# The four bit steps of a weight set apart, and the prologue's hand-written order rewritten

## The chip, the cores and the metric

The kernel runs on one core of one Trainium2 chip. The metric is the device time of one execution in microseconds (us), the median of three runs.

## What is computed

Windowed attention with a second, pooled branch (the reference's `_attn_ref`), whose output is the input of a gated feed-forward layer (`_moe_ref`):

```python
k_sum = k.reshape(B, H, nb, 32, D).max(axis=3)
v_sum = v.reshape(B, H, nb, 32, D).mean(axis=3)
scores_l = where(|row - column| < 16, scale * q @ k.T, -1e9)
scores_s = scale * q @ k_sum.T + log(32)
a = softmax(concat([scores_l, scores_s]))            # + 1e-9 in the divisor
x = a @ concat([v, v_sum])                           # 4 x 8 heads x 768 x 64
out = (silu(x @ w_gate) * (x @ w_val)) @ w_out       # 3072 tokens, 512 -> 1536 -> 512
```

The weights arrive as 64-bit floats. The kernel takes them as pairs of 32-bit words and makes 32-bit floats of them on the chip.

## The kernel before

The 3072 tokens are worked in eight blocks `k` of 384 tokens (half a batch each). Attention of a block has four units `u` (two heads each). The feed-forward layer of a block has twelve slices `j` of 128 of the 1536 inner columns. For each (k, j), `gate` and `val` (line 499, twelve matmuls each, three terms of a split of 32-bit floats into a high and a low part) lead over `silu`, `mul`, `ah` and `al` to `down` (line 550, nine matmuls that add to three banks of the block).

The weights are loaded and converted once, in a prologue that also does the attention of blocks 0 and 1 and the feed-forward layer of block 0 and half of block 1. Weight slice (j, gv) holds gate and value columns together (1024 per partition), (j, o) the output rows (512); slices 0 and 11 have `g` and `v` apart. A slice takes these steps: `w_load` (the transfer, SP queue), `w_abs` (ScalarE, line 177), `w_clamp` (two VectorE instructions, lines 185 and 187, the second on the result of the first), `w_bits` (two more, lines 195 and 198, each on the result of the one before), `w_hi` (a rounding copy, line 152 on ScalarE or line 154 on VectorE) and `w_lo` (a subtraction, line 148, on VectorE or, where the order says `=p`, on GpSimd).

Attention unit (k, u): keys, queries and values are loaded (`kt`, `q`, `kw`, `vn`, `vw`), keys pooled (`pool`) and windows put together (`winA`, `winB`, `join`), then `scores` (line 383), the running minimum `ttr0`/`ttr1` (line 398), `exp0`/`exp1` (line 413), `rcp` (lines 430 and 431), `nrm` (line 435), `tr0`/`tr1` (line 449), `pt0`/`pt1`, `out` (line 473), `split` and `rest`, which give the high and low part (`xh`, `xl`) of the layer's input. `first_values` (line 362) pools the first values on TensorE.

`PROLOGUE` (line 68) lists all these steps in one hand-written order; a suffix `=a`, `=d` or `=p` names ScalarE, VectorE or GpSimd. The loop at line 627 issues them so, and lines 632 to 635 tie every instruction to the one before it on its engine. So each engine, and the SP queue that starts the transfers, works through its part of the list strictly in order, and a step that has to wait holds all that stands behind it on that engine. After the prologue, `put_attention` and `do` (lines 648 to 677) place the attention of later blocks between the matmuls of the layer.

Of the kernel before, what the change touches and what calls it, by code (L numbers as in the profile page):

```python
# [98 lines left out]
w_clamp(7,o) down(1,0) w_hi(6,gv)=d mul(1,1) w_lo(6,gv)=d ah(1,1)=a gate(1,2) al(1,1)=d w_abs(8,gv)  # L99
w_clamp(4,gv) val(1,2) w_clamp(8,gv) silu(1,2) w_bits(4,gv) down(1,1) mul(1,2) w_hi(4,gv)=d ah(1,2)=a gate(1,3)  # L100
w_bits(8,gv) val(1,3) silu(1,3) al(1,2)=d w_hi(8,gv)=a w_lo(4,gv)=d down(1,2) w_lo(8,gv)=d w_abs(5,gv) mul(1,3)
w_abs(9,gv) w_clamp(5,gv) gate(0,4) ah(1,3)=a w_lo(4,o)=d al(1,3)=d w_bits(5,gv) val(0,4) silu(0,4) w_bits(7,o)
down(1,3) w_hi(5,gv)=a mul(0,4) w_hi(7,o)=a w_lo(5,gv)=d gate(1,4) ah(0,4)=d w_abs(7,gv) w_lo(7,o)=d al(0,4)=d
# [627 lines left out]
```

## Time and profile before

| | before |
|---|---|
| median of three runs | 726.92 us (726.63 to 727.62) |
| the profiled execution | 727.39 us, its span 725.6 us |
| TensorE busy | 705.6 us, 97% of the span |
| VectorE, ScalarE, GpSimd busy | 295.4, 319.0, 136.7 us |
| moved by DMA | 62.02 MB |

The span is cut in stretches and each engine's busy time read in each. A timeline row is one instruction (or several alike) with its start, its duration, its engine, line, operation and tiles; in square brackets stands how long the engine had been idle before it and on what it waited. "PEclk" is the granted clock of TensorE as a share of its full speed.

### The profile page before, as it was taken

Reading aid. Unit: us, or ns where it says so; the run is one execution under the profiler, and the core shown is the slowest. Engines: PE = TensorE matmul, PEld = TensorE weight load, DVE = VectorE, ACT = ScalarE, POOL = GpSimd, SP = SyncE. Lnnn points to the kernel's source line nnn. Section 1 sums busy time; section 2 is a strip of 40 time slices with the busy share of each in tenths; the row PEclk is TensorE's granted clock in tenths of the full one; section 3 lists DMA queues with packets and bytes.
Section 4 is the critical chain, followed back from the end, with each engine's and each line's share of the span. In section 5 each row is a group of like instructions: output and inputs, shape, how many; then the busy total and the mean of one; then the engine's idle time right before and its main releaser. Section 6 shows DMA issues by size and latency. Waiting matters only on the chain.

```text
span 725.6 us, 12513 instructions
## 1 busy us (share of the span) xinstructions
PE 705.6 (97%) x4986; PEld 642.9 (89%) x4986; DVE 295.4 (41%) x840; ACT 319.0 (44%) x779; POOL 136.7 (19%) x150
## 2 busy tenths in 40 slices
...
PEclk8798999999999999999999999999999999999999
...
GB/s 292 351 357 373 93 1 1 95 34 126 182 163 110 66 44 44 45 111 47 64 89 110 67 44 44 15 74 44 45 45 45 84 5 17 2 38 7 1 1 43
DMA packets 56522, 62.02 MB, mean 85 GB/s; under 512 B 24272, under 2 KB 46480, under 8 KB 55184
## 3 DMA queue, kind: packets, MB, share of 16 engines
...
## 4 chain that ended last, share of the span: by engine, by line
PE 82%; DVE 13%; ACT 2%; issue 1%; DMA 1%; SPq 0%; ACTq 0%; DVEq 0%
PE v L499 25%; PE g L499 24%; PE acc L550 24%; PE xo L473 3%; PE sc L383 3%; PE pp L449 2%; DVE m_gv L195 1%; DVE m_gv L198 1%; DMA vn<-in_vP 1%; DVE al L148 1%; PE pv L362 1%; DVE a L511 1%; DVE w_gv L148 1%; DVE m_gv L185 1%; DVE m_o L195 1%
## 5 line engine op out<-in xcount | busy, mean ns | idle before, releaser
L499 PE MATMUL g<-xh,w_gv 128*128 128x384 f32 x640 | 179.4, 341 | 3.3 <-DVE w_gv L148 3.1
L499 PE MATMUL v<-xh,w_gv 128*128 128x384 f32 x640 | 180.2, 342 | 1.1 <-DVE a L511 1.0
L550 PE MATMUL acc<-w_o,ah 128*128 128x512 f32 x576 | 179.3, 392 | 0.0
L511 DVE TENSOR_TENSOR a<-v,a 128x384 f32<-128x384 f32 x96 | 53.4, 556 | 251.0 <-PE v L499 250.9
L148 POOL TENSOR_TENSOR al<-a,ah 128x384 fp32r<-128x384 f32 x78 | 79.1, 1015 | 259.0 <-ACT ah L152 259.0
L550 PEld LDWEIGHTS acc<-w_o,ah 128*128 128x128 f32 x576 | 108.0, 188 | 20.2
L499 PEld LDWEIGHTS g<-xh,w_gv 128*128 128x128 f32 x640 | 118.3, 190 | 6.5 <-DVE w_gv L148 3.5
L499 PEld LDWEIGHTS v<-xh,w_gv 128*128 128x128 f32 x640 | 117.7, 189 | 5.2 <-issue 2.4
L550 PE MATMUL acc<-w_o,al 128*128 128x512 f32 x288 | 114.5, 398 | 0.7 <-DVE al L148 0.7
L506 ACT ACTIVATE a<-g 128x384 f32<-128x384 f32 x96 | 47.2, 492 | 143.3 <-PE g L499 141.9
L499 PE MATMUL g<-xl,w_gv 128*128 128x384 f32 x320 | 108.5, 339 | 0.0
L499 PE MATMUL v<-xl,w_gv 128*128 128x384 f32 x320 | 108.1, 338 | 0.0
L152 ACT CAST ah<-a 128x384 fp32r<-128x384 f32 x91 | 46.4, 509 | 121.4 <-DVE a L511 121.4
L413 ACT ACTIVATE p<-p,nm 128x120 f32<-128x120 f32 x192 | 73.2, 382 | 0.6 <-DVE nm L398 0.3
L550 PEld LDWEIGHTS acc<-w_o,al 128*128 128x128 f32 x288 | 54.0, 188 | 11.6 <-DVE al L148 1.6
L499 PEld LDWEIGHTS g<-xl,w_gv 128*128 128x128 f32 x320 | 60.7, 190 | 2.5
L435 POOL TENSOR_TENSOR p<-p,ri 128x720 f32<-128x720 f32 x29 | 40.6, 1401 | 108.0 <-DVE ri L431 106.5
L499 PEld LDWEIGHTS v<-xl,w_gv 128*128 128x128 f32 x320 | 60.5, 189 | 0.0
L506 ACT ACT_TABLE_LOAD x27 | 34.6, 1283 | 53.9 <-PE g L499 53.7
L154 POOL COPY kw<-ks 128x144 f32<-128x144 f32 x25 | 7.6, 304 | 194.1 <-DVE ks L277 118.8
L398 DVE CUSTOM_DVE_ANT_0 p<-sc,bias_sb 128x120 f32<-128x120 f32 x192 | 41.2, 277 | 1.6 <-PE sc L383 1.5
L499 PE MATMUL g<-xh,w_g 128*128 128x384 f32 x128 | 36.1, 343 | 0.0
...
## 6 DMA issues: line engine op xcount, KB each, us to landing
...
```

The source lines that it names most:

```text
L148: (nc.vector if e == "d" else nc.gpsimd).tensor_tensor(out=out, in0=a, in1=b.bitcast(F32), op=ALU.subtract)
L152: nc.scalar.copy(out, in_)
L195: nc.vector.scalar_tensor_tensor(out=f, in0=high, scalar=-0x40000000, in1=f, op0=ALU.bitwise_and, op1=ALU.bitwise_or)
L383: nc.tensor.matmul(sc[h][s * QT : (s + 1) * QT, c * KC : (c + 1) * KC], t["q"][hs, qs], t["kw"][hs, i, :], start=True, stop=True,)
L398: nc.vector.tensor_tensor_reduce(out=t["p"][:, i, :], in0=t["sc"][g][:, c * KC : (c + 1) * KC], in1=bias_sb[:, 0 if n == 0 else 2 if n == ...
L413: nc.scalar.activation(out=t["p"][:, i, :], in_=t["p"][:, i, :], func=AF.Exp, scale=-1.0, bias=t["nm"][:, i : i + 1], accum_out=t["sm"][:, ...
L435: (nc.vector if on == "d" else nc.gpsimd).tensor_tensor(out=p, in0=p, in1=ri.rearrange("p (n o) -> p n o", o=1).broadcast_to([P, NT, KC]), ...
L473: nc.tensor.matmul(ps[hs, qs], vw, t["pt"][:, h, qs], start=True, stop=True)
L499: nc.tensor.matmul(ps[:, :TOK], w[:, cs], x, start=u == 0 and n == 0, stop=u == NP - 1 and n == 2)
L506: nc.scalar.activation(out=a, in_=A.pop(("g", k, j))[:, :TOK], func=AF.Silu)
L511: nc.vector.tensor_tensor(out=a, in0=ps[:, :TOK], in1=a, op=ALU.mult)
L550: nc.tensor.matmul(ACC[k][i], a[:, ts], w, start=j == 0 and n == 0, stop=j == NJ - 1 and n == 2)
```

## The change

`w_clamp` and `w_bits` are cut into four steps of one instruction each (`w_clamp`, `w_shift`, `w_sign`, `w_low`), and the addition of 1e-9 leaves `rcp` for a step `eps` of its own. The instructions are the same; the list can now put other work between them. The whole list is new: what stands where, on which engine the movable steps run, and in which order the SP queue starts the transfers. A step `dummy` (idle matmuls) is defined and not used in the list, and the tile `warm` moves to another pool. What comes after the prologue is not touched. The list below is cut after the first third, and its end is shown.

```diff
 PROLOGUE = """
-kt(1) q(0,3) q(0,1) kt(3) pool(1) winA(1)=a winB(1)=p bias() mean() vn(0) join(0,1)=a scores(0,1) pool(3)
-winA(3)=a winB(3)=a vn(2) ttr0(0,1) join(0,3)=a scores(0,3) ttr1(0,1) exp0(0,1) first_values(0) odd1(0)=d id()
-kt(0) ttr0(0,3) odd2(1)=p odd1(1)=p ttr1(0,3) exp1(0,1) q(0,0) odd2(0)=d kt(2) odd1(2)=p first_values(2)
-odd2(3)=a rcp(0,1) odd1(3)=a fv_copy(0)=d kw(1,1) nrm(0,1)=p exp0(0,3) fv_copy(1)=d pool(0) w_load(0,g)
-val1(0,1)=a winB(0)=p tr0(0,1) exp1(0,3) join(0,0)=d winA(0)=d tr1(0,1) vw(1,0) pool(2) val1(0,0)=p scores(0,0)
-val2(0,1)=p pt1(0,1)=a q(0,2) winB(2)=p fv_copy(2)=d pt0(0,1)=a rcp(0,3) w_load(1,gv) odd2(2)=a join(1,1)=d
-out(0,1) join(0,2)=d nrm(0,3)=p winA(2)=a ttr0(0,0) w_abs(0,g) ttr1(0,0) exp0(0,0) w_clamp(0,g) tr0(0,3)
-tr1(0,3) split(0,1)=d val1(0,2)=p scores(0,2) fv_copy(3)=a kw(1,0) values(1,0)=p val2(0,0)=a pt1(0,3)=d
-val1(0,3)=a rest(0,1) w_load(0,v) val2(0,3)=p exp1(0,0) pt0(0,3)=d w_bits(0,g) out(0,3) w_abs(1,gv) q(1,0)
-w_load(3,gv) rcp(0,0) ttr0(0,2) join(1,0)=p w_hi(0,g)=a nrm(0,0)=p split(0,3)=a ttr1(0,2) exp0(0,2) rest(0,3)
-w_lo(0,g)=d scores(1,0) exp1(0,2) w_clamp(1,gv) w_load(2,gv) tr1(0,0) tr0(0,0) val2(0,2)=a rcp(0,2) pt1(0,0)=a
-ttr0(1,0) nrm(0,2)=p pt0(0,0)=a ttr1(1,0) w_abs(0,v) out(0,0) exp0(1,0) vw(1,2) w_bits(1,gv) tr0(0,2) q(1,1)
-exp1(1,0) tr1(0,2) w_load(2,o) pt0(0,2)=a rcp(1,0) pt1(0,2)=a w_clamp(0,v) q(1,2) w_hi(1,gv)=a out(0,2)
-w_load(0,o) nrm(1,0)=d values(1,2)=a w_bits(0,v) tr1(1,0) split(0,0)=a tr0(1,0) room(0) w_load(10,gv)
-split(0,2)=a scores(1,1) rest(0,0) w_lo(1,gv)=p pt1(1,0)=a w_hi(0,v)=a pt0(1,0)=d rest(0,2) gate(0,0) w_abs(2,o)
-ttr0(1,1) w_abs(0,o) ttr1(1,1) exp0(1,1) kw(1,3) w_lo(0,v)=d w_load(8,o) out(1,0) w_clamp(0,o) exp1(1,1)
-w_clamp(2,o) val(0,0) w_load(1,o) silu(0,0) rcp(1,1) w_bits(0,o) kw(1,2) w_abs(3,gv) split(1,0)=d nrm(1,1)=p
-gate(0,1) vw(1,1) mul(0,0) rest(1,0) w_abs(2,gv) w_load(5,o) w_clamp(3,gv) ah(0,0)=a val(0,1) silu(0,1)
-w_clamp(2,gv) w_load(8,gv) join(1,3)=a join(1,2)=a values(1,1)=a al(0,0)=d w_hi(0,o)=a tr1(1,1) w_bits(2,gv)
-tr0(1,1) w_abs(1,o) scores(1,2) pt0(1,1)=a q(1,3) pt1(1,1)=a w_load(6,o) out(1,1) mul(0,1) w_lo(0,o)=p
-w_hi(2,gv)=a ttr0(1,2) w_load(6,gv) ttr1(1,2) split(1,1)=a down(0,0) exp0(1,2) rest(1,1) w_lo(2,gv)=d
-w_bits(2,o) gate(0,2) w_load(7,gv) exp1(1,2) w_clamp(1,o) w_hi(2,o)=a rcp(1,2) w_bits(1,o) val(0,2) ah(0,1)=a
-silu(0,2) w_load(3,o) nrm(1,2)=d w_bits(3,gv) tr1(1,2) w_hi(1,o)=a w_load(4,gv) tr0(1,2) pt1(1,2)=a scores(1,3)
-pt0(1,2)=a out(1,2) w_lo(1,o)=d w_hi(3,gv)=a al(0,1)=d vw(1,3) ttr0(1,3) split(1,2)=a down(0,1) w_lo(3,gv)=d
-w_load(7,o) exp0(1,3) rest(1,2) w_load(9,o) gate(0,3) ttr1(1,3) values(1,3)=p mul(0,2) exp1(1,3) w_load(4,o)
-ah(0,2)=d w_lo(2,o)=d val(0,3) w_abs(6,gv) rcp(1,3) al(0,2)=d w_load(10,o) nrm(1,3)=d w_abs(3,o) w_abs(7,o)
-w_clamp(6,gv) w_load(5,gv) tr1(1,3) silu(0,3) tr0(1,3) down(0,2) w_clamp(3,o) pt0(1,3)=d w_abs(4,o) pt1(1,3)=d
-w_abs(4,gv) mul(0,3) out(1,3) w_load(9,gv) w_bits(3,o) ah(0,3)=a split(1,3)=a al(0,3)=d w_hi(3,o)=a rest(1,3)
-gate(1,0) w_clamp(4,o) val(1,0) w_lo(3,o)=d silu(1,0) w_bits(4,o) w_abs(6,o) w_clamp(6,o) w_hi(4,o)=a down(0,3)
-mul(1,0) w_bits(6,o) gate(1,1) ah(1,0)=d w_hi(6,o)=d al(1,0)=d w_lo(6,o)=d w_bits(6,gv) val(1,1) silu(1,1)
 ...
-w_clamp(10,gv) val(0,7) silu(0,7) w_bits(10,gv) down(0,6) mul(0,7) w_hi(10,gv)=d ah(0,7)=a gate(0,8)
-w_lo(10,gv)=d al(0,7)=d room(1) w_load(11,v) val(0,8) silu(0,8) w_load(11,o) down(0,7) w_load(11,g) mul(0,8)
-ah(0,8)=a w_abs(11,v) al(0,8)=d w_clamp(11,v) gate(0,9) w_abs(11,o) w_bits(11,v) w_abs(11,g) w_clamp(11,o)
-val(0,9) silu(0,9) w_clamp(11,g) w_hi(11,v)=d w_bits(11,g) down(0,8) w_lo(11,v)=d w_hi(11,g)=a mul(0,9)
-w_lo(11,g)=d ah(0,9)=a gate(0,10) w_bits(11,o) al(0,9)=d w_hi(11,o)=d val(0,10) silu(0,10) w_lo(11,o)=d
 ...
+kt(1) q(0,1) kt(3) q(0,3) pool(1) winB(1)=a winA(1)=p bias() mean() vn(2) join(0,1)=d scores(0,1) pool(3)
+winB(3)=a winA(3)=a join(0,3)=d scores(0,3) kt(0) ttr0(0,1) ttr1(0,1) exp0(0,1) q(0,0) kt(2) ttr0(0,3)
+first_values(2) odd2(3)=p ttr1(0,3) odd1(3)=p id() vn(0) odd1(2)=p pool(0) exp1(0,1) winB(0)=p winA(0)=d
+join(0,0)=p exp0(0,3) eps(0,1) scores(0,0) winB(2)=d rcp(0,1) q(0,2) fv_copy(2)=d nrm(0,1)=d fv_copy(3)=a
+kw(1,1) odd2(2)=a pool(2) val2(0,3)=p exp1(0,3) tr1(0,1) w_load(0,g) val1(0,2)=p tr0(0,1) val1(0,3)=p ttr0(0,0)
+first_values(0) odd1(0)=a odd1(1)=p pt1(0,1)=d pt0(0,1)=a q(1,0) odd2(1)=p ttr1(0,0) exp0(0,0) kw(1,0) odd2(0)=p
+eps(0,3) winA(2)=d w_load(1,gv) rcp(0,3) exp1(0,0) join(0,2)=d nrm(0,3)=d scores(0,2) fv_copy(1)=d join(1,1)=p
+w_abs(0,g) fv_copy(0)=d val2(0,1)=p tr0(0,3) val1(0,1)=a eps(0,0) w_clamp(0,g) tr1(0,3) val2(0,2)=a rcp(0,0)
+out(0,1) ttr0(0,2) val1(0,0)=p val2(0,0)=a q(1,2) nrm(0,0)=p pt1(0,3)=a pt0(0,3)=d w_load(0,v) exp0(0,2)
+ttr1(0,2) out(0,3) split(0,1)=d join(1,0)=p exp1(0,2) w_shift(0,g) w_load(2,o) rest(0,1) tr1(0,0) scores(1,0)
+w_sign(0,g) pt1(0,0)=a eps(0,2) vw(1,0) split(0,3)=a w_low(0,g) tr0(0,0) w_abs(1,gv) rcp(0,2) q(1,1) rest(0,3)
+nrm(0,2)=p ttr0(1,0) vw(1,2) w_hi(0,g)=a ttr1(1,0) pt0(0,0)=a w_load(3,gv) exp0(1,0) tr1(0,2) w_clamp(1,gv)
+out(0,0) w_lo(0,g)=d exp1(1,0) w_shift(1,gv) tr0(0,2) w_sign(1,gv) w_abs(0,v) w_load(0,o) pt0(0,2)=a eps(1,0)
+pt1(0,2)=a w_clamp(0,v) rcp(1,0) values(1,2)=a w_shift(0,v) out(0,2) w_load(2,gv) nrm(1,0)=d values(1,0)=a
+w_low(1,gv) split(0,0)=a tr1(1,0) tr0(1,0) split(0,2)=a scores(1,1) pt1(1,0)=a w_sign(0,v) pt0(1,0)=a rest(0,0)
+w_hi(1,gv)=a room(0) w_load(10,gv) out(1,0) w_low(0,v) w_abs(0,o) rest(0,2) w_lo(1,gv)=p gate(0,0) ttr0(1,1)
+split(1,0)=a w_hi(0,v)=a rest(1,0) exp0(1,1) ttr1(1,1) kw(1,2) w_clamp(0,o) exp1(1,1) w_load(8,o) w_lo(0,v)=d
+w_shift(0,o) val(0,0) w_abs(2,gv) eps(1,1) w_sign(0,o) kw(1,3) rcp(1,1) w_low(0,o) silu(0,0) w_load(1,o)
+nrm(1,1)=d w_clamp(2,gv) w_load(3,o) tr1(1,1) w_hi(0,o)=a gate(0,1) mul(0,0) join(1,2)=p join(1,3)=a
+w_shift(2,gv) w_abs(2,o) w_load(7,o) w_lo(0,o)=d ah(0,0)=a pt1(1,1)=a w_sign(2,gv) scores(1,2) w_abs(1,o)
+vw(1,1) silu(0,1) w_clamp(1,o) tr0(1,1) w_abs(3,gv) w_low(2,gv) q(1,3) val(0,1) w_load(4,gv) pt0(1,1)=a
+ttr0(1,2) al(0,0)=p w_abs(3,o) ttr1(1,2) w_hi(2,gv)=a values(1,1)=p down(0,0) mul(0,1) exp0(1,2) w_shift(1,o)
+w_lo(2,gv)=d w_load(9,gv) out(1,1) w_sign(1,o) w_clamp(3,gv) exp1(1,2) gate(0,2) w_low(1,o) w_load(10,o)
+w_shift(3,gv) split(1,1)=a w_hi(1,o)=a eps(1,2) rest(1,1) ah(0,1)=a val(0,2) rcp(1,2) w_sign(3,gv) w_load(7,gv)
+silu(0,2) nrm(1,2)=d al(0,1)=d w_abs(4,gv) tr1(1,2) w_low(3,gv) tr0(1,2) scores(1,3) w_load(5,gv) pt0(1,2)=a
+pt1(1,2)=d w_lo(1,o)=p w_hi(3,gv)=a mul(0,2) out(1,2) ttr0(1,3) ah(0,2)=a w_lo(3,gv)=p ttr1(1,3) down(0,1)
+exp0(1,3) split(1,2)=d vw(1,3) rest(1,2) w_load(4,o) w_clamp(2,o) gate(0,3) w_clamp(3,o) exp1(1,3) w_load(6,o)
+w_shift(2,o) al(0,2)=d w_sign(2,o) w_abs(5,gv) w_load(9,o) eps(1,3) w_low(2,o) val(0,3) values(1,3)=a rcp(1,3)
+w_shift(3,o) w_hi(2,o)=a nrm(1,3)=d w_load(6,gv) silu(0,3) w_lo(2,o)=d tr0(1,3) tr1(1,3) w_sign(3,o) down(0,2)
+pt0(1,3)=d w_abs(6,o) mul(0,3) pt1(1,3)=a w_low(3,o) w_load(8,gv) w_abs(10,o) ah(0,3)=d w_clamp(5,gv) out(1,3)
+w_hi(3,o)=a w_clamp(10,o) w_lo(3,o)=d split(1,3)=a w_shift(10,o) w_abs(4,o) rest(1,3) gate(1,0) w_load(5,o)
+al(0,3)=d w_shift(5,gv) val(1,0) silu(1,0) w_sign(10,o) w_sign(5,gv) w_clamp(6,o) down(0,3) w_low(5,gv)
+w_shift(6,o) w_hi(5,gv)=a mul(1,0) gate(1,1) w_sign(6,o) ah(1,0)=a w_low(10,o) w_low(6,o) w_hi(10,o)=a al(1,0)=d
 ...
+w_lo(10,gv)=d w_low(7,gv) w_abs(9,gv) val(1,5) al(0,5)=d silu(1,5) w_clamp(9,gv) w_hi(7,gv)=a w_shift(9,gv)
+down(0,5) mul(1,5) w_sign(9,gv) gate(0,6) w_lo(7,gv)=d w_low(9,gv) w_abs(8,gv) val(0,6) ah(1,5)=d silu(0,6)
+w_clamp(8,gv) w_hi(9,gv)=a al(1,5)=d w_shift(8,gv) down(1,5) w_lo(9,gv)=d w_sign(8,gv) room(1) w_load(11,g)
+gate(0,7) mul(0,6) w_load(11,o) w_low(8,gv) ah(0,6)=a al(0,6)=d w_hi(8,gv)=a val(0,7) w_load(11,v) w_abs(11,g)
+w_lo(8,gv)=d silu(0,7) w_abs(11,o) down(0,6) w_clamp(11,g) mul(0,7) w_shift(11,g) ah(0,7)=d w_abs(11,v)
+w_clamp(11,o) w_sign(11,g) gate(0,8) w_clamp(11,v) w_low(11,g) w_shift(11,v) w_shift(11,o) w_sign(11,v) val(0,8)
+silu(0,8) w_sign(11,o) al(0,7)=d w_low(11,o) w_hi(11,g)=d down(0,7) w_hi(11,o)=a w_low(11,v) w_lo(11,g)=d
+w_hi(11,v)=d mul(0,8) gate(0,9) w_lo(11,v)=d ah(0,8)=a w_lo(11,o)=d al(0,8)=d val(0,9) silu(0,9) down(0,8)
 ...
     def w_clamp(j, nm):
-        low, high, m = W[nm, j]
-        f = m.bitcast(I32)
+        m = W[nm, j][2]
         nc.vector.tensor_scalar(out=m, in0=m, scalar1=F64_LO, scalar2=F64_HI, op0=ALU.max, op1=ALU.min)
+    def w_shift(j, nm):
+        f = W[nm, j][2].bitcast(I32)
         nc.vector.tensor_scalar(
             out=f, in0=f, scalar1=3, scalar2=0x3FFFFFF8,
             op0=ALU.logical_shift_left, op1=ALU.bitwise_and,
         )
-    def w_bits(j, nm):
+    def w_sign(j, nm):
         low, high, m = W[nm, j]
         f = m.bitcast(I32)
         nc.vector.scalar_tensor_tensor(
             out=f, in0=high, scalar=-0x40000000, in1=f, op0=ALU.bitwise_and, op1=ALU.bitwise_or
         )
+    def w_low(j, nm):
+        low, high, m = W[nm, j]
+        f = m.bitcast(I32)
         nc.vector.scalar_tensor_tensor(
             out=f, in0=low, scalar=29, in1=f, op0=ALU.logical_shift_right, op1=ALU.bitwise_or
         )
 ...
+    def spare(ps):
+        nonlocal dummies
+        for _ in range(dummies):
+            nc.tensor.matmul(ps[:, TOK:], warm, warm, start=True, stop=True)
+        dummies = 0
+        return ps
 ...
+    def a_more(k, u):
+        sm = U[k, u]["sm"]
+        nc.vector.tensor_scalar(out=sm, in0=sm, scalar1=1e-9, scalar2=None, op0=ALU.add)
     def a_inverse(k, u):
-        sm, ri = U[k, u]["sm"], U[k, u]["ri"]
-        nc.vector.tensor_scalar(out=sm, in0=sm, scalar1=1e-9, scalar2=None, op0=ALU.add)
-        nc.vector.reciprocal(out=ri, in_=sm)
+        nc.vector.reciprocal(out=U[k, u]["ri"], in_=U[k, u]["sm"])
 ...
     def a_norm(k, u):
+        a_more(k, u)
         a_inverse(k, u)
         a_scale(k, u)
 ...
-    warm = pro.tile([P, P], F32, name="warm")
+    warm = dec.tile([P, P], F32, bufs=1, name="warm")
 ...
```

## Rows read from the trace of the kernel before

**Rows 1.** Page, busy time by engine, and TensorE's granted clock in 40 slices.
```profile
PE 705.6 (97%) x4986; PEld 642.9 (89%) x4986; DVE 295.4 (41%) x840; ACT 319.0 (44%) x779; POOL 136.7 (19%) x150
...
PEclk8798999999999999999999999999999999999999
```
**Rows 2.** Busy by stretch: length, PE, PEld, DVE, ACT, POOL, PEclk, DMA share, GB/s.
```profile
18.00:58.20 40.20, 29.72 (x352) 24.33 (x351) 38.89 (x116) 33.62 (x92) 12.72 (x11) 0.87 1.02 359
58.20:135.00 76.80, 75.53 (x438) 69.29 (x438) 73.78 (x131) 37.66 (x73) 0.00 (x0) 0.96 0.27 90
...
171.00:725.60 554.60, 550.62 (x3884) 505.40 (x3882) 148.57 (x518) 228.60 (x567) 118.90 (x126) 1.00 0.20 60
```
**Rows 3.** Timeline of TensorE: pauses ahead of the layer's matmuls.
```profile
39.41 0.45 PE L499 MATMUL g<-xl,w_g 128*128 128x384 f32 x1 [1.11 <-DVE xl L148]
...
58.27 0.69 PE L499 MATMUL g<-xh,w_gv 128*128 128x384 f32 x1 [3.10 <-DVE w_gv L148]
...
119.59 0.44 PE L499 MATMUL v<-xh,w_gv 128*128 128x384 f32 x1 [0.81 <-DVE a L511]
```
**Rows 4.** TensorE by stretch: length, busy, granted clock, DMA share, GB/s.
```profile
17.30:27.20 9.90, 6.14 (x132) 0.99 1.06 354
27.20:36.90 9.70, 7.85 (x66) 0.50 1.05 342
...
58.20:64.00 5.80, 5.73 (x18) 0.50 1.07 287
```
**Rows 5.** Timeline of VectorE: pairs that depend, and what follows them.
```profile
42.01 0.42 DVE L185 TENSOR_SCALAR m_o<-m_o 128x512 f32<-128x512 f32 x1
42.47 0.43 DVE L187 TENSOR_SCALAR m_o<-m_o 128x512 int32<-128x512 int32 x1
42.81 0.42 DVE L185 TENSOR_SCALAR m_o<-m_o 128x512 f32<-128x512 f32 x1
...
86.75 1.22 DVE L195 SCALAR_TENSOR_TENSOR m_gv<-raw_gv,m_gv 128x1024 int32<-128x1024 int32 x1
88.00 1.23 DVE L198 SCALAR_TENSOR_TENSOR m_gv<-raw_gv,m_gv 128x1024 int32<-128x1024 int32 x1
89.14 0.42 DVE L185 TENSOR_SCALAR m_o<-m_o 128x512 f32<-128x512 f32 x1
```
**Rows 6.** Timelines of GpSimd and VectorE from 34.9 to 38.9 us.
```profile
34.95 2.66 POOL L148 TENSOR_TENSOR w_gv<-m_gv,w_gv 128x1024 fp32r<-128x1024 f32 x1 [3.86 <-ACT w_gv L152]
...
35.30 2.85 DVE L195 SCALAR_TENSOR_TENSOR m_v<-raw_v,m_v 128x512 int32<-128x512 int32 x1
38.19 0.69 DVE L198 SCALAR_TENSOR_TENSOR m_v<-raw_v,m_v 128x512 int32<-128x512 int32 x1
```
**Rows 7.** Groups by line and form, first 182 us: count, busy, mean ns, idle before.
```profile
L152 ACT CAST w_gv<-m_gv 128x1024 fp32r<-128x1024 f32 x7 | 7.4, 1053 | 12.3 <-DVE m_gv L198 12.3
L413 ACT ACTIVATE p<-p,nm 128x120 f32<-128x120 f32 x48 | 18.3, 382 | 0.1
L435 DVE TENSOR_TENSOR p<-p,ri 128x720 f32<-128x720 f32 x3 | 2.7, 902 | 0.0
L148 POOL TENSOR_TENSOR w_o<-m_o,w_o 128x512 fp32r<-128x512 f32 x1 | 1.3, 1316 | 4.4 <-ACT w_o L152 4.4
```
**Rows 8.** Stations: VectorE's timeline, and one piece of the chain that ended last.
```profile
39.73 0.55 DVE L148 TENSOR_TENSOR xl<-xo,xh 128x384 fp32r<-128x384 f32 x1
...
57.01 1.21 DVE L148 TENSOR_TENSOR w_gv<-m_gv,w_gv 128x1024 fp32r<-128x1024 f32 x1
...
138.07 2.08 PE g L499 x12
```
**Rows 9.** Timelines of TensorE, ScalarE and SP: waits for transfers, and a late issue.
```profile
11.06 6.23 PE L362 MATMUL pv<-vn,mean_sb 128*24 128x128 f32 x56 [1.07 <-DMA vn<-in_vP]
...
13.10 1.03 ACT L152 COPY vw<-vn 32x384 f32<-32x384 f32 x2 [2.08 <-DMA vn<-in_vP]
...
138.43 0.33 SPq L168 DMA_DIRECT2D raw_g<-in_wgv  x1
```

More of the change, by code (lines that the diff above doesn't have):

```diff
@@ L99 @@
[L99 to L103, printed above, removed]
@@ L104 @@
-w_abs(9,o) w_clamp(9,gv) val(1,4) silu(1,4) w_abs(5,o) w_clamp(9,o) w_abs(8,o) w_clamp(5,o) down(0,4)
-w_bits(9,o) w_bits(5,o) gate(0,5) mul(1,4) w_hi(5,o)=d ah(1,4)=a w_hi(9,o)=d w_lo(5,o)=d val(0,5) silu(0,5)
-w_lo(9,o)=d al(1,4)=d w_abs(10,o) w_clamp(8,o) down(1,4) w_clamp(10,o) mul(0,5) w_bits(8,o) ah(0,5)=a gate(1,5)
-al(0,5)=d w_hi(8,o)=d w_bits(10,o) val(1,5) silu(1,5) w_lo(8,o)=d w_hi(10,o)=a w_clamp(7,gv) w_lo(10,o)=d
-down(0,5) w_bits(7,gv) gate(0,6) mul(1,5) w_hi(7,gv)=a w_bits(9,gv) ah(1,5)=a val(0,6) silu(0,6) al(1,5)=d
@@ L109 @@
-w_hi(9,gv)=a w_lo(7,gv)=d down(1,5) mul(0,6) w_lo(9,gv)=d gate(0,7) ah(0,6)=d w_abs(10,gv) al(0,6)=d
-w_clamp(10,gv) val(0,7) silu(0,7) w_bits(10,gv) down(0,6) mul(0,7) w_hi(10,gv)=d ah(0,7)=a gate(0,8)
-w_lo(10,gv)=d al(0,7)=d room(1) w_load(11,v) val(0,8) silu(0,8) w_load(11,o) down(0,7) w_load(11,g) mul(0,8)
-ah(0,8)=a w_abs(11,v) al(0,8)=d w_clamp(11,v) gate(0,9) w_abs(11,o) w_bits(11,v) w_abs(11,g) w_clamp(11,o)
-val(0,9) silu(0,9) w_clamp(11,g) w_hi(11,v)=d w_bits(11,g) down(0,8) w_lo(11,v)=d w_hi(11,g)=a mul(0,9)
@@ L114 @@
-w_lo(11,g)=d ah(0,9)=a gate(0,10) w_bits(11,o) al(0,9)=d w_hi(11,o)=d val(0,10) silu(0,10) w_lo(11,o)=d
-down(0,9) mul(0,10) ah(0,10)=a al(0,10)=d load(2,0) gate(0,11) val(0,11) silu(0,11) down(0,10) mul(0,11)
-ah(0,11)=d al(0,11)=d down(0,11)
+kt(1) q(0,1) kt(3) q(0,3) pool(1) winB(1)=a winA(1)=p bias() mean() vn(2) join(0,1)=d scores(0,1) pool(3)
+winB(3)=a winA(3)=a join(0,3)=d scores(0,3) kt(0) ttr0(0,1) ttr1(0,1) exp0(0,1) q(0,0) kt(2) ttr0(0,3)
+first_values(2) odd2(3)=p ttr1(0,3) odd1(3)=p id() vn(0) odd1(2)=p pool(0) exp1(0,1) winB(0)=p winA(0)=d
```

27 lines of the change are left out of this document (22 added, 5 removed).

## The prediction

> **What bounds the kernel now.** Read the engines' busy times first: TensorE works through 97% of the span [rows 1], so only its pauses and its slow stretches are to be had. Next, the stretches [rows 2]: behind 171 us it is busy for 550.6 of 554.6 us at full clock, and of those 4 us nearly all is the drain at the very end. The change touches nothing there. From 58.2 to 135 us it pauses for 1.3 us in all. What can be won lies ahead of 58.2 us: in 18.0 to 58.2 TensorE is busy for only 29.7 of 40.2 us, while VectorE is busy for 38.9. Then the pauses themselves [rows 3]: the slice-2 gate waits 3.10 us for a VectorE subtraction (w_lo of weight slice 2), the first gate 1.11 us for VectorE's `xl`. Last, the clock [rows 4]: behind the 3.10 us pause it stands at 0.50, which is 1.2 GHz, up to 64 us, so 5.73 us of work would have been 2.9. It also stood at 0.50 from 27.2 to 36.9, in a stretch of short pieces of attention.
>
> So VectorE, in its fixed order, decides how early TensorE's unbroken row of matmuls begins. I count that with one number, V: the time at which `gate(0,0)` would have begun had TensorE run from there without pause and at full clock. A gate, val or down takes 2.08 us [rows 8], and I take 0.85 us for an `out` and 0.77 for six transposes or a `scores`, estimates from their spacing at full clock. `gate(0,7)` stands at 138.07 [rows 8], and the list has 86.2 us of TensorE's work between it and `gate(0,0)`: V = 51.9 before. The prologue's whole work from `gate(0,0)` is 119.5 us, so it ends at 171.4, where the trace has it. In the new list one `out` more stands ahead of `gate(0,0)`, so 118.6 us follow.
>
> **Part 1: steps set apart.** In [rows 5] a 512-wide instruction is followed after 0.46 us by one that needs its result, and the next, which doesn't, begins 0.34 us after that. With the 1024-wide pair it is 1.25 against 1.14. So a dependent neighbour costs 0.11 to 0.12 us on VectorE. Going through both lists, I count 70 such neighbours on VectorE in the old one (clamp and bits of 26 slices, the eight `rcp`, and some others) and 7 in the new one. 63 x 0.12 = 7.6 us less VectorE time by the end of the prologue; 17 of the 63, 2.0 us, lie ahead of slice 2's w_lo. TensorE, ScalarE and GpSimd don't run these instructions, so nothing else changes by it. What stands between the pairs is other VectorE work that has to be done anyway; where that work is not ready, the in-order queue waits for it and the gain of that pair is gone.
>
> **Part 2: who does what.** Between the engines the new list takes 6 of 9 `w_hi`, net 2 `w_lo`, and some small copies from VectorE, and gives it three more `nrm` at 0.82 each (the 0.90 us of [rows 7] less the overlap with the next). Added up at start-to-start times this is 3.4 us less. The whole VectorE prologue is 142.4 us of work by the old list and 131.5 by the new. `w_hi` goes to ScalarE, which has the room (busy 37.7 of 76.8 us in [rows 2]). The `w_lo` of slices 1, 3 (both gv), 1 and 8 (both o) are GpSimd's. What that costs is seen in [rows 6]: GpSimd's 2.66 us subtraction begins at 34.95, and VectorE's bit instruction at 35.30, elsewhere 0.69 us, takes 2.85. It stood still until GpSimd was done. So such a step on GpSimd costs VectorE between 0 (where what comes next reads PSUM, as the running minimum does) and its full length, 2.66 or 1.32 us [rows 6, 7].
>
> **Part 3: the order, followed along VectorE.** *Transfers.* The new list sends vn(2) in the place of vn(0) and moves the other vn behind kt(0), q(0,0), kt(2). The first vn landed at 11.06, the second, 800 KB, at 13.1 [rows 9], at some 0.36 to 0.39 MB per us [rows 2, 9]. So kt(0) lands at about 12.2, kt(2) at 13.9, vn(0) at 16.3 instead of 11.06. Only `first_values(0)` and the values of units 0 and 1 need vn(0), and half of the 6.23 us of [rows 9] is its price: done at 19.5 to 20, about when VectorE comes to its copies.
>
> *To the last `xl` of block 0* (`rest(0,2)`). From `pool(0)`, at 12.2, VectorE has 22.75 us of work to it in the new list. I find three short waits on the way (kt(2), an `exp` row of three times 0.38 [rows 7], one `w_abs`), 0.9 us: 35.9. Before it ended at 40.28 [rows 8]. The old and the new list have the same amount of VectorE work up to here; the difference is the 2.2 us lost in [rows 6], which now come later, and about 2 us of earlier waits.
>
> *To `val(0,0)`.* It needs w_lo(0,v), 2.6 us later in VectorE's work. GpSimd's w_lo(1,gv) runs at 36.2 to 38.9, and VectorE stands still in `w_clamp(0,o)` until then: 39.9. TensorE is there at 38.3 and waits 1.6 us.
>
> *To `gate(0,2)`.* 10.6 us of VectorE work to w_lo(2,gv), and two short GpSimd steps that I let block in full, 1.0 and 0.8: 52.2. TensorE arrives at 51.0 to 51.2. Before, 58.27. The 3.10 us stall is gone but for about 1 us, and it stood in front of 2.9 us of clock loss.
>
> *To `gate(0,3)`.* Its weight goes a longer way now: 6.6 us on VectorE to `w_low(3,gv)`, 1.3 us of standing behind GpSimd's w_lo(1,o): 60.1; 1.05 us of `w_hi` on ScalarE [rows 7]; 2.66 us on GpSimd: 63.9. TensorE, which has waited some 2 us for `nrm(1,2)` ahead of the transposes, is there at 63.5. With 21.4 us of its work since `gate(0,0)` that is V = 42.5. This is what is late next: slice 3, in place of slice 2.
>
> *Behind it.* VectorE's clock time is then ahead of its summed work by 13.4 us, with w_lo(8,o) on GpSimd 14.7. The tightest later weight is w_lo(8,gv): 118.05 us of summed work, so 132.7, and 91.6 us of TensorE's work from `gate(0,0)`: V = 41.1, under 42.5, so it fits with 1.4 us to spare. Against that stand two unknowns. Another 0.50 clock stretch behind one of the pauses (1.6, 2 us): 0 to 2.6 us. And slice 11: the old raw_g was held until 138.43 [rows 9], when VectorE had done with a tile in whose place it goes; now w_load(11,v) is last and may be held until w_lo(8,gv). Its clamp would then hold `al(0,7)` and TensorE for up to 2 us. I take 1.8 us for both, nearer to the middle: V = 44.3.
>
> **The sum.** 51.9 + 119.5 = 171.4 before; 44.3 + 118.6 = 162.9 after: 8.5 us less. From the profiled execution's 727.4: 718.9; the median of the runs lies 0.5 lower, so 718.5 us.
>
> **Rivals.** *(a) GpSimd blocks in full.* I let its steps cost 3.8 us of VectorE up to slice 8; if all five (1.0, 0.8, 1.3, 2.66, 1.3) block from end to end it is 7.1, and V rises by 3.3: 722. For it speaks [rows 6], against it that PSUM readers stand next to the two long ones. 14%.
>
> *(b) Setting apart buys nothing.* If the gaps in [rows 5] were owed to the kind of instruction and not to the dependence, the 53 pairs ahead of w_lo(8,gv) would give back 6.3 us, that weight would set V at 47.4, with the allowance above 48.5, and the time would be about 723. Against it stands that in [rows 5] the same instruction, 185, begins 0.34 us after its independent neighbour and 187 0.46 after a 185 that it depends on. 6%. The Trainium skill, VectorE: DVE Perf Modes, section "The DRAIN you can't avoid", says that the next VectorE operation doesn't start before the pipe is empty, and that it pays to have fewer operations, not fewer waits. By that rule this rival is the forecast; the overlap of 0.08 us at 42.81 in the trace speaks against it.
>
> *(c) The transfer of slice 2 decides.* w_load(2,gv) stands 1.7 MB later in the SP queue, behind 11.1 MB. At the 359 GB/s of [rows 2] it lands near 36, and its conversion takes 7 us from there. If a held tile ahead of it on SP keeps it until 50, `gate(0,2)` is where it was, and the time about 726.5. 5%.
>
> *(d) Slower: the low clock.* The new order has TensorE pause in four places near the layer's first gates (1.6, 1, 2 and 0.4 us) instead of one of 3.1. If the clock falls to 1.2 GHz behind each and stays there as long as behind the 3.10 us pause, that is 4 x 2.6 = 10.4 us, more than the 8.5 won: 729. It decides from the fourth such stretch. Against it: the 1.11 us pause of [rows 3] was followed by no fall, and pauses totalling 3.8 of the 9.9 us from 17.3 to 27.2 left the granted clock at 0.99 there [rows 4], though it fell right after. 5%.
>
> **How the numbers follow.** Forecast, V from 41 to 47 and 715 to 721.5: 62%. Better, with TensorE held by nothing but w_lo(2,gv) and V of 39.5 to 41: 714 to 715, 8%. (a) 14%, (b) 6%, (c) 5%, (d) 5%. The range leaves out (c), (d) and some of (b): 714 to 724. A measurement of this kernel tells about 0.2%, 1.5 us, from no change. Faster by more than that: all but (c) and (d), 90%; within it 5%; slower 5%.
>
> **What would show it.** In the profile after: no pair of lines 185/187 or 195/198 of one tile side by side on VectorE; `rest(0,2)` near 36, `gate(0,2)` near 52, `gate(0,3)` near 64 behind a GpSimd subtraction of 2.66 us; the first stretch behind which TensorE has no pauses ending near 163 instead of 171. The forecast is wrong if the gates come early and a later weight (slice 8 or 11) opens a new pause, if TensorE shows 0.50 behind `gate(0,0)` for more than 6 us, or if the first `xl` of block 0 are no earlier than before.

## The result, and the profile after

The changed kernel takes 717.55 us (median of four runs, 715.42 to 718.25) where the kernel before takes 726.77 in the same runs: a ratio of 0.9877, 95% interval 0.9863 to 0.989. Measured again later, beside other kernels, it took 716.88 us, ratio 0.9884 (0.9864 to 0.9903). The profiled execution took 718.11 us, its span 716.3, 9.3 us less than the span before.

The page of the kernel after: busy time by engine, and the granted clock in 40 slices. They answer to [rows 1].

```profile
PE 699.2 (98%) x4986; PEld 638.4 (89%) x4986; DVE 283.5 (40%) x832; ACT 322.4 (45%) x782; POOL 140.0 (20%) x155
...
PEclk9899999999999999999999999999999999999999
```

VectorE's busy time has gone from 295.4 to 283.5 us, TensorE's from 705.6 to 699.2 for the same 4986 matmuls: some of what it had been "busy" with was low clock. The stretches of the kernel after, columns as in [rows 2]:

```profile
18.00:58.20 40.20, 33.18 (x375) 27.42 (x371) 37.94 (x109) 37.35 (x101) 11.23 (x11) 0.95 1.03 360
58.20:135.00 76.80, 76.58 (x452) 70.77 (x451) 74.39 (x132) 41.44 (x69) 3.68 (x2) 0.98 0.36 111
...
171.00:716.30 545.30, 541.34 (x3818) 496.53 (x3810) 143.24 (x512) 226.38 (x563) 117.13 (x123) 1.00 0.20 57
```

From 18 to 58.2 us TensorE is busy 3.5 us longer than before, from 58.2 to 135 another 1.0, and behind 171 us it pauses for 4.0 us as it did. VectorE is as full as before (37.94 of 40.2, 74.39 of 76.8). TensorE's pauses ahead of the layer's matmuls, which answer to [rows 3]:

```profile
38.79 0.45 PE L522 MATMUL v<-xh,w_v 128*128 128x384 f32 x1 [0.41 <-DVE w_v L154]
...
51.27 0.45 PE L522 MATMUL g<-xh,w_gv 128*128 128x384 f32 x1 [0.25 <-DVE w_gv L154]
...
57.21 0.84 PE L472 MATMUL pp<-id_sb,p 128*120 128x128 f32 x6 [1.44 <-DVE p L457]
```

The slice-2 gate begins at 51.27 with a wait of 0.25, where it began at 58.27 with one of 3.10. What is late next is `nrm(1,2)`, which holds the transposes for 1.44 us. The pairs on VectorE, which answer to [rows 5]:

```profile
30.14 0.42 DVE L190 TENSOR_SCALAR m_v<-m_v 128x512 f32<-128x512 f32 x1
30.48 0.18 DVE L453 RECIPROCAL ri<-sm 128x6 f32<-128x6 f32 x1
30.59 0.43 DVE L195 TENSOR_SCALAR m_v<-m_v 128x512 int32<-128x512 int32 x1
...
111.00 1.22 DVE L203 SCALAR_TENSOR_TENSOR m_gv<-raw_gv,m_gv 128x1024 int32<-128x1024 int32 x1
112.14 0.55 DVE L154 TENSOR_TENSOR al<-a,ah 128x384 fp32r<-128x384 f32 x1
112.60 0.69 DVE L190 TENSOR_SCALAR m_gv<-m_gv 128x1024 f32<-128x1024 f32 x1
113.21 1.22 DVE L210 SCALAR_TENSOR_TENSOR m_gv<-raw_gv,m_gv 128x1024 int32<-128x1024 int32 x1
```

A clamp is followed after 0.34 us by a reciprocal of another unit, the sign step after 1.14 by another tile's subtraction. Each step begins before the one ahead of it has ended.

With the prediction's number V (start of a gate or down, less TensorE's work since `gate(0,0)` at full clock) the traces compare station by station. Each value is the start of that step's first matmul in the timeline, less that sum:

```
                gate(0,0)  val(0,0)  gate(0,2)  gate(0,3)  gate(1,0)  gate(0,7)  down(0,10)
before            37.9       39.5      44.7       48.1       48.1       51.7       51.7
after             36.0       36.7      38.5       42.6       42.6       43.2       43.2
after, again      36.3       37.0      38.8       41.4       41.4       42.0       42.0
x1_joined         36.3       37.3      40.2       43.0       43.4       47.7       48.1
x2_old_apart      38.2       39.2      44.4       46.6       46.6       49.3       49.3
x3_vn_early       39.5       40.7      44.4       47.0       47.0       47.6       47.6
x5_no_pool        36.2       37.3      38.9       40.0       41.2       41.8       41.8
x6_join_late      36.5       37.2      39.0       41.6       41.8       46.2       46.5
x6b_join_early    35.5       36.9      39.4       42.3       42.4       43.0       43.0
x7_new_head       35.7       36.5      38.4       42.4       42.5       44.2       44.3
```

Between before and after, 5.5 us are won by `gate(0,3)` and 3.0 more by `gate(0,7)`: 8.5 in all. One `out` more stands ahead of `gate(0,0)` in the new list and adds 0.85, which makes the 9.3 us of the spans. These are single executions; two of the changed kernel differ by 1.2 us.

### The profile page after: what moved, and what is told of

It is laid out like the page before. It is cut to its first block, busy times and chain, and to the rows that moved or that the text cites. A ratio compares the mean times of both kernels' runs of the same rounds, so it can differ in the third digit from the quotient of the medians.

```text
span 716.3 us, 12534 instructions
## 1 busy us (share of the span) xinstructions
PE 699.2 (98%) x4986; PEld 638.4 (89%) x4986; DVE 283.5 (40%) x832; ACT 322.4 (45%) x782; POOL 140.0 (20%) x155
## 4 chain that ended last, share of the span: by engine, by line
PE 92%; DVE 3%; DMA 3%; ACT 1%; issue 1%; SPq 0%; ACTq 0%
PE acc L573 27%; PE v L522 27%; PE g L522 27%; PE xo L496 3%; PE sc L403 3%; PE pp L472 3%; DMA kt<-in_kP 2%; DMA raw_o<-in_wo 1%; DVE m_gv L203 0%; DVE p L418 0%; PE pv L382 0%; ACT p L433 0%; DVE m_gv L210 0%; DVE p L457 0%; PE pv L372 0%
## 5 line engine op out<-in xcount | busy, mean ns | idle before, releaser
L154 POOL TENSOR_TENSOR al<-a,ah 128x384 fp32r<-128x384 f32 x79 | 81.1, 1026 | 265.3 <-ACT ah L158 265.3
L457 POOL TENSOR_TENSOR p<-p,ri 128x720 f32<-128x720 f32 x26 | 36.2, 1391 | 98.1 <-DVE ri L453 98.0
L418 DVE CUSTOM_DVE_ANT_0 p<-sc,bias_sb 128x120 f32<-128x120 f32 x192 | 41.4, 276 | 0.7 <-PE sc L403 0.7
L522 PE MATMUL v<-xh,w_v 128*128 128x384 f32 x128 | 36.1, 342 | 0.4 <-DVE w_v L154 0.4
## 6 DMA issues: line engine op xcount, KB each, us to landing
raw_gv<-in_wgv SPq DMA_DIRECT2D x10, 1024.0 KB, 12.2
```

The source lines that it names most:

```text
L154: (nc.vector if e == "d" else nc.gpsimd).tensor_tensor(out=out, in0=a, in1=b.bitcast(F32), op=ALU.subtract)
L418: nc.vector.tensor_tensor_reduce(out=t["p"][:, i, :], in0=t["sc"][g][:, c * KC : (c + 1) * KC], in1=bias_sb[:, 0 if n == 0 else 2 if n == ...
L457: (nc.vector if on == "d" else nc.gpsimd).tensor_tensor(out=p, in0=p, in1=ri.rearrange("p (n o) -> p n o", o=1).broadcast_to([P, NT, KC]), ...
L522: nc.tensor.matmul(ps[:, :TOK], w[:, cs], x, start=u == 0 and n == 0, stop=u == NP - 1 and n == 2)
```

## The experiments

All differ from the changed kernel in its list alone. All ratios are to the kernel before, measured beside the kernel in question; the changed kernel is at 0.9877 and 0.9884. The kernel before itself had medians of 725.25 to 726.77 us in these measurements, so a ratio tells more than a difference of two medians, and both are given where they disagree.

**x1_joined.** The pairs are put together again in the new order (two of them shown):

```diff
-eps(0,0) w_clamp(0,g)
 tr1(0,3) val2(0,2)=a
+eps(0,0)
 rcp(0,0)
...
 split(0,1)=d join(1,0)=p exp1(0,2)
+w_clamp(0,g)
 w_shift(0,g)
```

> The new order with the pairs put together again: each clamp is moved down to directly ahead of its shift, each sign step ahead of its low step, each eps ahead of its reciprocal. Theory A (a dependent neighbour costs VectorE 0.12 us, and VectorE's queue sets TensorE's start): VectorE is 1.9 us later at the w_lo of slice 2, 2.5 us at the low step of slice 3, 6.6 us at the w_lo of slice 8; the slice-2 gate moves from 51.3 to about 53, the end of the prologue by 1.5 to 4 us, the time to 719 to 721.5 us. Theory B (the new order alone did it, the gaps between pairs are owed to the instruction's kind): no row of a pair changes its spacing and the time stays at 717.5 us.

It took 723.24 us, ratio 0.9969 (0.9958 to 0.998): of the 9.2 us won 5.7 are gone by the medians, 6.2 to 6.7 by the ratios. Theory B falls. But theory A had 1.5 to 4 us, mostly for an earlier start. In the table the start is little later (43.0 at `gate(0,3)`, against 42.6 and 41.4 in the two traces of the changed kernel, the first of which had lost clock just ahead of it); 5.1 us are lost behind it. VectorE's timeline, then TensorE's, of this kernel, at the largest single loss:

```profile
121.67 1.22 DVE L200 SCALAR_TENSOR_TENSOR m_gv<-raw_gv,m_gv 128x1024 int32<-128x1024 int32 x1
122.92 1.23 DVE L207 SCALAR_TENSOR_TENSOR m_gv<-raw_gv,m_gv 128x1024 int32<-128x1024 int32 x1
124.06 0.55 DVE L151 TENSOR_TENSOR al<-a,ah 128x384 fp32r<-128x384 f32 x1
```

```profile
116.48 0.50 PE L570 MATMUL acc<-w_o,al 128*128 128x512 f32 x1 [0.68 <-DVE al L151]
...
124.67 0.51 PE L570 MATMUL acc<-w_o,al 128*128 128x512 f32 x1 [1.62 <-DVE al L151]
```

The pair's second begins 1.25 us behind its first again. What TensorE waits for there is no weight but `al`, which stands in VectorE's queue behind the bit steps.

**x2_old_apart.** The old order, the second of each pair moved behind the next independent VectorE step:

```diff
-w_clamp(0,g) tr0(0,3) tr1(0,3) split(0,1)=d
+w_clamp(0,g) tr0(0,3) tr1(0,3) split(0,1)=d w_shift(0,g)
```

> The old order, with nothing changed but that the second of each pair is moved behind the next independent VectorE step (58 of 60; about 40 dependent neighbours fewer, 15 of them ahead of the w_lo of slice 2). Theory A: VectorE is 1.8 us earlier at the w_lo of slice 2 (gate at 56.5 instead of 58.3) and 4.2 us earlier at the w_lo of slice 7, so that the end of the prologue moves by 3 to 4.5 us: 722 to 724 us. Theory B (setting apart gives nothing without the new order): 726.8 us.

725.09 us, ratio 0.9999 (0.999 to 1.0009): nothing, and theory A's 2 to 4 us are not there. (This edit takes about 40 of the gaps away, where the new list has 63 fewer.) In its trace the slice-2 gate still waits:

```profile
58.05 0.44 PE L519 MATMUL g<-xh,w_gv 128*128 128x384 f32 x1 [3.05 <-DVE w_gv L151]
```

VectorE's subtraction ahead of it began at 56.78, against 57.01 in [rows 8], though fifteen gaps were gone. VectorE's own waits from 18 to 58 us in this kernel (who waited for whom, total us, times, longest) show part of where they went. Behind them stands the only wait of VectorE in that stretch of the trace before, for a weight's `abs`:

```profile
DVE sm L447 <- ACT p L430: 1.2, 3, 0.6
DVE xl L151 <- ACT xh L155: 0.3, 1, 0.3
```

```profile
DVE m_g L185 <- ACT m_g L177: 0.4, 1, 0.4
```

The eps step now waits for ScalarE's `exp`. And one sign step lasts 2.12 and one 2.18 us, where its own length is 1.22, because a GpSimd instruction began just ahead of it. The second, GpSimd and VectorE:

```profile
50.11 1.45 POOL L151 TENSOR_TENSOR w_o<-m_o,w_o 128x512 fp32r<-128x512 f32 x1 [4.04 <-ACT w_o L155]
```

```profile
50.46 2.18 DVE L200 SCALAR_TENSOR_TENSOR m_gv<-raw_gv,m_gv 128x1024 int32<-128x1024 int32 x1
```

Added up from the rows between 18 and 58 us, VectorE's instructions beside GpSimd's last 5.7 us longer than the same ones do elsewhere in the trace before, 6.5 us in this one, and 2.0 us in the changed kernel's. So the gaps had been covering waits, and the new order does away with most of this standing still, of which the prediction had read only the 2.2 us of [rows 6]. What that is worth in time was not tested by itself. In this trace the prologue ended 2.4 us earlier than in that of before; the medians give 0.5, so the one profiled execution of before lay high.

**x6_join_late and x6b_join_early.** x1's edit on the pairs behind `gate(0,3)` alone, and on those ahead of it alone.

```diff
-w_clamp(8,gv) w_hi(9,gv)=a al(1,5)=d w_shift(8,gv)
+w_hi(9,gv)=a al(1,5)=d w_clamp(8,gv) w_shift(8,gv)
```

(x6_join_late; one of its pairs. For x6b_join_early the lines shown for x1 are two.)

> The new order with only the pairs behind the slice-3 gate put together again (43 more dependent neighbours; the 18 ahead of it stay apart). Theory L (in x1_joined the start was 0.4 us later at the slice-3 gate and lost 4.5 us behind it, so the steps set apart pay where TensorE runs without a pause and VectorE must keep up): 721.5 to 723 us. Theory A as predicted (they pay by an earlier start, and behind it VectorE has 1.4 us to spare): at most 719 us.

> The new order with only the 18 or so pairs ahead of the slice-3 gate put together again. Theory L (the early pairs are covered by waits for ScalarE and GpSimd, as they were in x2_old_apart, where VectorE's w_lo of slice 2 came only 0.2 us earlier): at most 1 us more than the changed kernel. Theory A as predicted (2.5 us of VectorE time ahead of slice 3 go straight into the start): 2 to 2.5 us more. Together with x6_join_late it should make up the 5.7 us that x1_joined lost.

Late pairs together: 721.41 us, ratio 0.9945 (0.9929 to 0.9961), 0.68% or 4.9 us over the changed kernel's; 43 gaps of 0.12 us make 5.2. Early pairs together: 718.38 us, ratio 0.9896 (0.9876 to 0.9915), 1.5 us over the changed kernel's median of 716.88 measured beside it, but 0.12% or 0.9 us by the ratios; the runs of the two overlap, so this is not told apart from nothing. It is less than the 2 to 2.5 us of theory A, and theory L's 1 us is not excluded. The late ones are as L had them. The two make up x1's 0.9% but for 0.1%. TensorE's timeline with the late pairs together shows the same wait as x1:

```profile
114.92 0.50 PE L570 MATMUL acc<-w_o,al 128*128 128x512 f32 x1 [0.71 <-DVE al L151]
...
123.11 0.51 PE L570 MATMUL acc<-w_o,al 128*128 128x512 f32 x1 [1.62 <-DVE al L151]
```

**x7_new_head.** The new list up to `gate(1,0)`, then the rest in the old order, pairs apart:

```diff
 w_shift(10,o) w_abs(4,o) rest(1,3)
-gate(1,0) w_load(5,o) al(0,3)=d w_shift(5,gv) val(1,0) silu(1,0) w_sign(10,o)
+w_load(5,o) w_shift(5,gv) al(0,3)=d gate(1,0) w_clamp(4,o) val(1,0) w_shift(4,o)
...
```

> The new list up to gate(1,0), then what is left in the order of the old list with its pairs set apart (and its choice of engines; slices 5 and 6 gv and 7 and 10 o are exchanged in it, since the head leaves 5 and 10 half done). Theory L (the rest of the list must keep up too; the old rest lost 2.8 us behind gate(1,0) even with the pairs apart): 719.5 to 721 us. Rival (the head is all that counts once the pairs are apart): 717.5 us within 0.7.

719.12 us, ratio 0.9907 (0.9878 to 0.9936): 0.2 to 0.3% over the changed kernel, just under theory L's range and above the rival's. The interval reaches down to the changed kernel, but every run (717.97 to 719.33) lies above all those of x5 and x8, measured beside it (716.26 to 717.04). Its rest also has net six `w_hi` back on VectorE, so order and engines are not told apart in these 0.2 to 0.3%. From x2, which has the same rest but for the exchanged slices, the new head alone takes 0.92% off, 6.7 us.

**x3_vn_early.** The transfer of vn(0) back to where the old list had the pair of them; `id`, a small one, goes with it:

```diff
 vn(2)
+vn(0) id()
...
 kt(0)
...
 q(0,0) kt(2)
...
-id() vn(0)
```

> The new order, with the transfer of vn(0) put back directly behind vn(2), ahead of kt(0), q(0,0), kt(2) and id, as in the old list; no other step is moved. Theory A (from the pooling of unit 0 on VectorE is a packed queue, so an earlier kt(0) was worth its full time): kt(0) lands 2 to 2.4 us later, the first gate begins near 38 instead of 36.0, the time is 719 to 719.8 us. Theory C (later waits take it up): the first gate and the time stay within 0.5 us, 717.5 us.

721.35 us, ratio 0.994 (0.992 to 0.9961): 0.6% over the changed kernel, 3.8 us by the medians, more than theory A's 1.5 to 2.3 us. But its runs lie apart: two at 719.4 and 719.5, in theory A's range, three at 721.4 to 722.5, and the profiled one is the slowest. So theory A is right in kind, and the size is 0.4 to 0.6%. VectorE's pooling of unit 0 in the changed kernel, then in this one:

```profile
11.54 0.95 DVE L297 TENSOR_REDUCE ks<-kt 128x24 f32<-128x768 f32 x1 [0.45 <-DMA kt<-in_kP]
```

```profile
14.34 0.95 DVE L294 TENSOR_REDUCE ks<-kt 128x24 f32<-128x768 f32 x1 [2.72 <-DMA kt<-in_kP]
```

The pooling comes 2.8 us later, and the first gate 3.5 us later. So the order of these transfers carries 0.4 to 0.6 of the 0.92% that the head won.

**x5_no_pool.** GpSimd's weight steps on VectorE:

```diff
-w_lo(1,gv)=p
+w_lo(1,gv)=d
...
-al(0,0)=p
+al(0,0)=d
...
-w_lo(1,o)=p
+w_lo(1,o)=d
...
-w_lo(3,gv)=p
+w_lo(3,gv)=d
...
-w_lo(8,o)=p
+w_lo(8,o)=d
```

> The new order with the w_lo of slices 1 and 3 (gv), 1 and 8 (o) and al(0,0) on VectorE instead of GpSimd, in the same places of the list. That is 4.0 us more VectorE work (1.14 + 1.14 + 0.6 + 0.6 + 0.47); the trace of the new kernel shows VectorE standing still behind these five for 1.8 us (0.36 and 0.61 behind al(0,0), 0.83 behind w_lo(1,o)). Theory A (VectorE's queue is what counts, so GpSimd's part is worth the difference): 1.5 to 2.2 us more, 719 to 719.8 us. Rival (what GpSimd takes off it gives back by standing in the way): 717.5 us within 0.5.

716.55 us, ratio 0.9875 (0.9847 to 0.9904): by the ratio no difference, as the rival had it. The interval alone would leave room for theory A's 1.5 to 2.2 us; that all four runs (716.26 to 717.03) lie under A's range speaks against it, and so does the trace, whose V of 41.8 is under both of the changed kernel's. 4.0 us of VectorE work were given to GpSimd for nothing that shows.

**x4_dummy, x8_dummies, x9_both.** Idle matmuls in TensorE's waits: the three shown in x8, the last of them alone in x4, the first two in x9, there together with x5's edit:

```diff
+dummy(5)
 tr1(0,2)
...
+dummy(5)
 out(0,2)
...
+dummy(6)
 tr1(1,2)
```

> The new order, with six idle matmuls (about 1.3 us) ahead of the transposes of unit (1,2), where TensorE waits 1.44 us and its granted clock then falls to 0.50 from about 59.5 to 62.5 us. Theory D (the fall follows the pause, and costs about 1.5 us of the time): no 0.50 stretch there, the slice-3 gate begins 1 to 1.5 us earlier, 716 to 716.5 us. Rival: the slice-3 gate is held by its weight anyway (ready at 62.2) or the idle matmuls run into the transposes: 717.5 us or up to 0.5 us more.

> The new order with idle matmuls in three waits of TensorE: five ahead of the first transposes of unit (0,2) (wait 1.56 us), five ahead of the values of (0,2) (1.52 us), six ahead of the transposes of (1,2) (1.44 us). Theory D (the 1.2 GHz stretches from 30 to 36 and 59.5 to 62.5 us follow these waits, and cost 1 to 2.5 us in the executions that have them): 715 to 716.3 us, the granted clock over the span at 0.997 or more. Rival (VectorE sets these stations, a faster TensorE only waits longer): 717.0 us within 0.6.

> The new order with the five GpSimd steps on VectorE (as in x5_no_pool) and five idle matmuls each ahead of the first transposes and of the values of unit (0,2). In the two traces that have one of these alone the prologue ended 1.4 us earlier than in that of the changed kernel, but their medians are within 1 us of it. Theory D (each takes a part of the slow and of the blocked time, and the two add): 714.5 to 716 us, 0.2 to 0.4% under the changed kernel in this call. Rival (the traces differ by the luck of the clock, VectorE's queue sets the stations): within 0.15% of it.

x4 took 716.95 us, ratio 0.9879 (0.9859 to 0.9899); x8 716.77, ratio 0.9878 (0.985 to 0.9906); x9 716.24, ratio 0.9868 (0.9845 to 0.989), 0.09% under the changed kernel measured beside it by the medians, 0.16% by the ratios. None is told apart from the changed kernel, and none reached the range of theory D. In x4's trace the clock stayed up behind the wait, but it had been low ahead of the first gate, which began only at 37.42. x8 did what it was built for. Its stretches (length, PE, PEld, DVE, ACT, POOL, PEclk, DMA share, GB/s):

```profile
18.00:36.00 18.00, 14.92 (x241) 12.12 (x242) 17.23 (x60) 17.50 (x54) 5.03 (x7) 1.00 1.07 338
58.20:64.00 5.80, 5.58 (x67) 4.70 (x67) 5.77 (x22) 5.59 (x17) 2.39 (x1) 1.00 1.06 298
```

In this execution the granted clock over the whole span was 1.0, against 0.992 to 0.998 in the first four runs of the changed kernel, and the time was the same.

**x10_after.** The changed kernel again.

> The changed kernel again, to stand beside the others of this call on the same chip. All theories: 0.986 to 0.989 of the kernel before.

716.88 us, ratio 0.9884 (0.9864 to 0.9903), as expected. Its trace serves below.

## Why the prediction was right, step by step

The time lay 1 us under the forecast of 718.5, and V was 43.2 for 44.3. Not every step that led there held.

**The walk along VectorE held.** `rest(0,2)` ended at 35.1 (forecast 35.9), val(0,0) began at 38.79 (39.9), the slice-2 gate at 51.27 (52.2): each about 1 us early, one behind the other. kt(0) landed at 11.5 for 12.2, and x3 shows that this order of transfers matters: 0.4 to 0.6%.

**The slice-3 gate came at 63.92 for 63.9, but not for the reason given.** That the two agree is luck. The step failed: "its weight goes a longer way now". GpSimd's subtraction was over at 62.2:

```profile
59.83 2.38 POOL L154 TENSOR_TENSOR w_gv<-m_gv,w_gv 128x1024 fp32r<-128x1024 f32 x1 [4.66 <-ACT w_gv L158]
```

TensorE was not there yet. It had paused 1.44 us for `nrm(1,2)` and then run at 1.2 GHz. TensorE's stretches (length, busy, granted clock, DMA share, GB/s) in this execution:

```profile
55.60:57.20 1.60, 0.17 (x1) 1.00 1.02 422
57.20:59.60 2.40, 2.16 (x32) 0.92 1.02 376
59.60:62.50 2.90, 2.90 (x28) 0.50 1.10 248
```

In the second execution, x10, the same wait was 1.45 us, the clock stayed up, and the gate began at 62.74:

```profile
58.20:64.00 5.80, 5.58 (x67) 4.58 (x66) 5.77 (x22) 5.42 (x16) 2.41 (x1) 1.00 1.06 326
```

**The 1.8 us allowed behind it were 0.65** (42.56 to 43.21), and even these are no lost time: between `gate(0,3)` and `gate(0,7)` a gate or val takes 2.11 us in this trace and in x10's, not 2.08, and there are ten of each. Slice 11 cost nothing: raw_v was sent at 127.83, ahead of the w_lo of slice 8 at 131.67. VectorE's w_lo of slice 9 was over at 127.77, so by the times it was this tile that raw_v had waited for, and not the one I feared.

```profile
127.83 0.33 SPq L174 DMA_DIRECT2D raw_v<-in_wgv  x1
```

**"What can be won lies ahead of 58.2 us" was wrong**, and the sum came out because V was read at `gate(0,7)`. In the trace before, V was 48.1 at `gate(0,3)` already and rose to 51.7 by `gate(0,7)`; I had read the 1.3 us of idle time of [rows 2, 3] as all that was lost there. Pauses of TensorE were 0.81 and less, and the rest stood nowhere as idle. The changed kernel's V rises by the 0.65 above. So, in these two traces, 3.0 of the 8.5 us were won behind the slice-3 gate.

**Part 1 was right in kind and wrong in place.** The 7.6 us of gaps are real (x1: 5.7 to 6.7 us of time). But "17 of the 63, 2.0 us, lie ahead of slice 2" was counted as gain at the start, and those early pairs are worth 0.9 to 1.5 us in the new order (x6b), not told apart from nothing; in the old one (x2) slice 2 came only 0.2 us earlier, since the time went into waits for ScalarE and GpSimd. The step failed that put w_lo(8,gv) as "the tightest later weight" with 1.4 us to spare: it looked at weights alone. `al(1,4)` and `al(0,5)` stand in the same queue, and with the late pairs together TensorE waits for them 0.7 and 1.6 us. The old rest loses time there even with its pairs apart (V rises by 2.7 in x2, 1.8 in x7); in both `al(1,4)` is late, by 0.68 and 0.47 us, and the remainder was not traced.

**Part 2 was mis-sized.** The five GpSimd steps were to hold VectorE for 3.8 us, up to slice 8. The rows after show 1.8, and a third of that is owed to another step: the copy `values(1,1)`, which GpSimd did right behind `al(0,0)`. GpSimd, then VectorE, whose low step takes 1.22 us elsewhere, and so does its sign step:

```profile
46.08 0.91 POOL L160 COPY vw<-vs 24x768 f32<-24x768 f32 x1
53.87 1.29 POOL L154 TENSOR_TENSOR w_o<-m_o,w_o 128x512 fp32r<-128x512 f32 x1 [6.88 <-issue]
```

```profile
46.23 1.84 DVE L210 SCALAR_TENSOR_TENSOR m_gv<-raw_gv,m_gv 128x1024 int32<-128x1024 int32 x1
...
54.19 2.06 DVE L203 SCALAR_TENSOR_TENSOR m_gv<-raw_gv,m_gv 128x1024 int32<-128x1024 int32 x1
```

The long ones, 2.40 and 2.38 us, fell where VectorE read PSUM or waited anyway, and cost nothing. x5 shows no gain from the shift to GpSimd. The larger part of the 3.4 us, the `w_hi` that went to ScalarE, was not tested by itself.

**The rivals.** (a) falls with x5: the blocking is half of what I took, and taking it away changes nothing that shows. (b) falls with x1, whose pairs stand 1.25 us apart again where the changed kernel's steps of that width follow after 1.14. By the rule that the Trainium skill, VectorE: DVE Perf Modes, section "The DRAIN you can't avoid", states, that the next operation doesn't start before the pipe is empty, x1 would have equalled the changed kernel; the rows after and the 5.7 us between the two decide against it here. The section itself adds that "a next op that is not held starts earlier", so what falls is the rule taken alone. (c) falls: the slice-2 gate waited 0.25 us. (d) falls in its size: behind `gate(0,0)` one such clock stretch was in the trace after, none in x10's. Both had a slow stretch ahead of it too (0.72 from 30 to 36 us); x8, without either, is no faster.

**What the change is worth, by its parts** (ratios to before): the old order with pairs apart 0.9999, the new order with pairs together 0.9969, both 0.988. Neither part alone gives a third of the gain. With the pairs apart, the new head is worth 0.92% (x2 to x7), 0.4 to 0.6% of it by x3's measure the order of the transfers, and the new rest, with its engines, 0.2 to 0.3%. Why the order of the transfers cost 3.8 us by the medians in x3 where the pooling came 2.8 us later is open; the transfers of that trace also made one `out` wait 1.73 us for its values.
